# Stores of turned input-gradient leaf rows: from the SyncE queue to the GpSimd queue, with the order of all work planned anew

## The chip, the cores and the metric

The kernel runs on one core of a Trainium2 chip. The metric is the device time in microseconds (us) of one execution, the median of several runs. A core has five engines that work side by side, each through its own instructions in order: TensorE (PE: matmuls; its weight loads are listed as PEld), VectorE (DVE), ScalarE (ACT), GpSimd (POOL) and SyncE (SP). SP computes nothing: it issues transfers (DMAs) between the main memory and the on-chip memory. GpSimd can compute and can issue transfers as well. Whoever issues a transfer, 16 DMA engines of the core carry it out. Instructions of different engines wait for one another through semaphores; an instruction that waits holds up all that stand behind it on its engine.

## The reference

The reference is a strided 1-D convolution with group normalisation over time and GELU, and its gradients for all four inputs. With batch 2, time 16000, 256 channels in and out, K = 31 taps, stride 2 and L = 7985 output rows:

```python
h = sum(einsum('blc,cd->bld', x[:, i:i + 2 * L:2, :], w[i]) for i in range(31))
mu = h.sum(1) / L;  var = ((h - mu) ** 2).sum(1) / L
out = gelu(((h - mu) / sqrt(var + 1e-5)) * gn_gamma + gn_beta)      # tanh form
d_x, d_w, d_gamma, d_beta = vjp(out)(grad_out)
```

All arrays are bfloat16. The outputs are `out` and the four gradients.

## The kernel before

**Less multiplication, more addition.** The 31 taps, padded to 32, are split by nested sums and differences (three products where four would be needed, at several levels). A branch is called A, B or C at each level, and a pair of branch and leaf names one of nine leaf operands (`COMBOS`, L23). VectorE makes sums and differences of operand rows, TensorE multiplies leaf operands with leaf weights, ScalarE and VectorE spread and add partial results in PSUM.

**Stages.** F0 and F1 are the forward for batch 0 and batch 1 (`forward`, L908). GELU and its derivative for batch 0 (`gelu_batch`, L1063) run beside F1, those for batch 1 beside the first part of the input gradient. G0 and G1 are the input gradient for batch 0 up to its third chunk, and from its fourth chunk on (`input_grad`, L1453). W is the weight gradient (`weight_grad`, L1688). There are 4 chunks per batch, two halves (`pr`) per chunk in G, and three branches per half.

**The input gradient.** For each chunk `e_load` (L1205) loads the derivative rows (`dy_d`, in the trace `dyd`) and the forward's rows (`h_d`, `hd`); `e_comp` (L1213) turns them into the gradient before normalisation and spreads it into one of two buffers `ET`, with copies of a few halo columns on GpSimd (L1258) and memsets (L565). `g_sums` (L1284) makes the nine leaf operands of the chunk from it, matmuls (`g_mm`, L1335) use them, and `g_evac` (L1429) collects the result for a store to `out_1`.

**What the change touches.** The weight gradient needs the same nine leaf operands, but with time on the partitions. `dl_turn` (L1268) therefore turns each leaf by two transposing DMAs of 128 KB (`turn`, L558; in the trace L561, `arena<-arena`) into one of four row buffers `DNO` (L603), and stores the buffer's two halves with two DMAs of 128 KB in pieces of 512 bytes (`load`, L548; in the trace L556, `dld<-arena`) to the DRAM tensors `dl_d` (`dld`). Nine leaves in eight chunks make 72 leaves, 144 turns and 144 stores. `dl_turn` asks for GpSimd ("POOL"), but `load` overrides that: every transfer above 4096 bytes in a stage of `ONE`, which lists all stages, is issued by SP. The four buffers rotate, so the turns of a leaf wait until the stores of the leaf four earlier have landed. In W `d_tile` (L1561) loads those rows back.

**What else SP issues in these stages.** The loads of `e_load`; for GELU of batch 1, the loads of `hd`, the turns of `grad_out`, and the stores of `dyd` and `yd` (`gelu_unit`, L1100), where the buffer of `yd` is written again by ScalarE's L1110 in the next unit; the stores to `out_1`; and, towards the end, the first loads of `x` for W (L1541).

**What sets the order.** Nothing is emitted where it is written. `add` (L294) records every operation with its engine, an estimated duration, and the cells that it reads and writes. `order` (L323) gives each a due time: the place of the matmul that needs it, less durations, less a hand-kept lead for its kind (`lead`, and by chunk `fine`). `listing` (L341) then plays the engines through with the estimated costs, eight transfer slots for SP and eight for GpSimd among them, picks on each engine the ready operation that is due first, and `emit` (L465) issues all operations in the order of the starts that it found. A changed cost or lead can therefore move any instruction on any engine.

Of the kernel before, what the change touches and what calls it, by code (L numbers as in the profile page):

```python
# [12 lines left out]
ACT = mybir.ActivationFunctionType  # L13
# [25 lines left out]
class Plan:  # L39
# [3 lines left out]
    def __init__(self, tc):  # L43
# [10 lines left out]
            "F0 f_evac last": -14.5,  # L54
            "F0 f_mm f_leaf": -67.5,
            "F0 f_mm f_outer": 14.0,
            "F0 f_mm f_three_ac": -19.0,
            "F0 f_mm f_three_b": 56.0,
            "F0 f_mm pe_turn": -135.5,
            "F0 f_outer forward": -15.5,  # L60
            "F0 f_seed forward": -60.0,
            "F0 f_three_b f_first": -19.5,
            "F0 load f_evac": 62.5,
            "F0 load put": 10.5,
            "F0 tt f_sums": -97.0,
            "F0 tt second": 16.5,
            "F0 ve_neg f_seed": -25.0,
            "F0 w_sub f_first": 8.0,
            "F0 w_sum w2_part": 5.0,
            "F0 zero x_load": 16.5,  # L70
            "F1 f_evac last": -54.0,
            "F1 f_mm f_leaf": -235.5,
            "F1 f_mm f_three_ac": -3.5,
            "F1 f_mm f_three_b": -20.5,
            "F1 f_outer forward": 3.5,
            "F1 f_seed forward": 3.0,
            "F1 keep f_evac": 0.5,
            "F1 load f_evac": 60.5,
            "F1 load gelu_unit": 44.5,
            "F1 load out0_store": 57.0,  # L80
            "F1 tiny elem_finalize": 50.5,
            "F1 tiny fwd_stats": -72.0,
            "F1 tt f_sums": -41.0,
            "F1 tt gelu_unit": -21.0,
            "F1 tt second": -47.5,
            "F1 tt third": -63.5,
            "F1 turn gelu_batch": 21.5,
            "F1 turn gelu_unit": -5.0,
            "F1 turn x_load": 48.5,
            "F1 ve f_seed": -19.0,  # L90
            "G0 cp e_comp": 4.5,
            "G0 g_mm g_three_b": -9.0,
            "G0 g_three_b input_grad": 6.5,
            "G0 gelu_batch conv_stem_kernel": 3.5,
# [3 lines left out]
            "G0 load dgb_store": -3.5,  # L98
            "G0 load dl_turn": 8.0,
            "G0 load e_load": 22.5,  # L100
            "G0 load g_evac": 9.5,
            "G0 load load_w2": 29.5,
            "G0 plus g_seed": 5.0,
            "G0 tiny elem_finalize": -9.0,
            "G0 tt first": -48.0,
            "G0 tt gelu_unit": -0.5,
            "G0 tt second": 1.0,
            "G0 tt third": -113.0,
            "G0 turn dgb_store": 7.0,
            "G0 turn dl_turn": 1.0,  # L110
            "G0 turn gelu_batch": 5.5,
            "G0 w_sum load_w2": -47.0,
            "G0 zero e_comp": 7.0,
            "G0 zero gelu_batch": -54.0,
            "G1 cp e_comp": -94.5,
            "G1 e_comp e_load": 13.0,
            "G1 g_mm g_leaf": -2.0,
            "G1 g_mm g_outer": -7.5,
            "G1 g_mm g_three_ac": -8.0,
            "G1 g_mm g_three_b": -18.0,  # L120
            "G1 g_three_b input_grad": -201.5,
            "G1 keep g_evac": 3.5,
            "G1 keep g_seed": -2.0,
            "G1 load dl_turn": 11.0,
            "G1 load e_load": -6.0,
            "G1 load g_evac": -4.0,
            "G1 plus g_seed": 2.5,
            "G1 spread e_comp": -11.0,
            "G1 spread g_seed": -197.5,
            "G1 tt first": 3.5,  # L130
            "G1 tt second": -15.0,
            "G1 tt third": -13.0,
            "G1 turn dl_turn": 3.5,
            "G1 w_sum w2_outer": -21.5,
            "G1 zero e_comp": 1.0,
            "W keep w_keep": 4.5,
            "W keep weight_grad": 1.0,
            "W load d_tile": -32.5,
            "W load out0_late": 35.5,
            "W load w_emit": 13.5,  # L140
            "W load weight_grad": 39.0,
            "W load x_raw": 1.5,
            "W pair_d weight_grad": -3.5,
            "W pair_x weight_grad": 0.5,
            "W turn out0_late": -50.0,
            "W ve w_done": 8.5,
# [4 lines left out]
            "W w_emit w_done": 3.0,  # L151
            "W w_emit weight_grad": -196.0,
            "W w_mm w_leaf": 6.0,
            "W w_pairs weight_grad": -424.0,
# [5 lines left out]
            "F0 f_evac last": {0: 17.5, 3: -12.5},  # L160
            "F0 f_mm f_outer": {0: 37.5, 1: -12.5, 2: -135.0, 3: -49.5},
            "F0 f_mm f_three_ac": {0: -27.5, 1: -38.0, 2: -88.5},
            "F0 f_mm f_three_b": {0: 8.0, 1: -29.0, 2: -39.0, 3: -181.0},
            "F0 f_outer forward": {3: -15.0},
            "F0 f_seed forward": {3: 33.0},
            "F0 f_three_b forward": {0: -13.5},
            "F0 load f_evac": {2: 52.0, 3: -30.5},
            "F0 load put": {0: 22.0, 3: 20.5},
            "F0 tt f_sums": {0: -9.5, 1: 73.5, 2: 18.0},
            "F0 tt second": {1: -52.0, 2: -50.5},  # L170
            "F0 tt third": {1: 42.0, 2: -34.5, 3: 14.5},
            "F0 turn x_load": {0: 58.0, 2: 30.0},
            "F0 ve f_first": {0: -21.5},
            "F0 ve f_seed": {0: 24.0, 3: 1.0},
            "F0 ve_neg f_seed": {0: 88.5, 3: 58.5},
            "F0 w_sum w2_part": {1: 20.5, 2: 22.5},
            "F0 zero x_load": {3: 11.0},
            "F1 f_evac last": {3: -17.5},
            "F1 f_mm f_outer": {3: -41.0},
            "F1 f_mm f_three_ac": {1: -60.5, 3: -4.0},  # L180
            "F1 f_mm f_three_b": {2: 17.0},
            "F1 f_outer forward": {3: -9.5},
            "F1 f_seed forward": {3: 5.5},
            "F1 gelu_unit gelu_batch": {0: -26.0, 1: -15.0, 2: -22.0, 3: -74.0, 5: 11.5},
            "F1 keep f_evac": {3: 12.5},
            "F1 load f_evac": {3: -19.0},
            "F1 load gelu_unit": {2: 13.0, 3: -10.5, 5: -21.0, 6: -68.5},
            "F1 load out0_store": {0: 15.5, 1: 33.0, 2: 20.0, 3: 11.5, 4: -148.0, 5: -4.5, 6: 10.0, 7: 29.5},
            "F1 tiny elem_finalize": {0: -92.5},
            "F1 tiny fwd_stats": {0: 62.5},  # L190
            "F1 tt f_sums": {0: 3.0, 1: 46.0, 2: 30.0},
            "F1 tt gelu_unit": {2: 22.0, 4: 11.5},
            "F1 tt second": {0: -38.0, 2: 31.5},
            "F1 tt third": {3: 11.0},
            "F1 turn gelu_batch": {0: -185.0, 1: -49.0, 2: 30.5, 3: -58.0},
            "F1 turn gelu_unit": {0: -22.5, 1: -25.5, 2: -148.0, 3: -45.0, 5: 31.5, 6: -51.5, 7: -2.5},
            "F1 turn x_load": {1: 15.0, 2: 40.0, 3: -40.0},
            "F1 ve f_seed": {3: 29.0},
            "F1 w_sub f_again": {3: -37.5},
            "F1 zero f_evac": {3: -3.0},  # L200
            "G0 cp e_comp": {0: -151.0, 2: -2.5},
            "G0 e_comp e_load": {0: -17.5, 1: -8.0, 2: -8.5, 3: 7.0},
            "G0 g_mm g_leaf": {0: -2.0, 3: -173.5},
            "G0 g_mm g_three_ac": {1: -1.0, 3: 17.5},
            "G0 g_mm g_three_b": {0: -4.5, 1: 1.5, 2: -3.0},
            "G0 g_three_b input_grad": {0: 1.0, 1: 0.5, 3: 0.5},
            "G0 gelu_batch conv_stem_kernel": {6: 41.0},
            "G0 gelu_unit gelu_batch": {1: -8.0, 2: -3.0, 3: 2.5, 4: -7.0, 5: -4.5, 6: -3.0},
            "G0 keep g_evac": {0: -14.5, 2: -2.0},
            "G0 keep g_seed": {0: -4.0, 1: -1.5, 2: -1.0, 3: 2.5},  # L210
            "G0 load dgb_store": {0: -2.5},
            "G0 load dl_turn": {0: -28.0, 1: 1.5, 2: -8.5},
            "G0 load e_load": {0: -11.0, 1: -12.0, 2: 3.5},
            "G0 load g_evac": {0: -5.0},
            "G0 load gelu_unit": {0: 49.0, 1: 13.0, 2: 8.5, 3: -15.5, 5: -4.5, 6: -15.0},
            "G0 load load_w2": {3: -9.0},
            "G0 plus g_seed": {0: -2.5},
            "G0 spread e_comp": {0: 8.0, 1: -99.5, 2: 2.5, 3: -23.0},
            "G0 tiny elem_finalize": {0: 1.5},
            "G0 tt first": {2: 36.5},  # L220
            "G0 tt gelu_unit": {0: -36.5, 1: -1.5, 2: -40.0, 3: -10.0, 5: 2.5, 6: 2.0},
            "G0 tt second": {0: -72.0, 1: 7.0},
            "G0 tt third": {0: 99.5},
            "G0 turn dgb_store": {0: -5.5},
            "G0 turn dl_turn": {1: 1.0, 2: -2.0},
            "G0 turn gelu_batch": {0: 12.5, 2: 14.5, 3: 9.0, 4: -32.5, 5: 11.0, 6: -89.5, 7: -0.5},
            "G0 w_sum load_w2": {3: 24.5},
            "G0 zero e_comp": {2: 1.5, 3: 16.5},
            "G1 e_comp e_load": {1: 0.5},
            "G1 g_mm g_leaf": {0: -114.5, 3: -2.5},  # L230
            "G1 g_mm g_outer": {0: -8.5, 1: -9.0, 2: -2.5, 3: -1.5},
            "G1 g_mm g_three_ac": {0: -6.5, 1: -7.0, 2: -4.0, 3: -1.0},
            "G1 g_mm g_three_b": {0: 3.5, 1: 15.0, 2: 10.0, 3: 11.0},
            "G1 keep g_evac": {0: 1.5, 1: -1.0, 2: 4.5, 3: 1.0},
            "G1 load dl_turn": {0: -3.5, 1: -1.5},
            "G1 load e_load": {1: -2.0, 2: -0.5},
# [1644 lines left out]
```

## Time and profile before

| What | Value |
|---|---|
| Median of 3 runs | 1195.17 us (1194.51 to 1196.55) |
| Profiled execution, its own time | 1190.87 us |
| Its span, first to last instruction | 1189.1 us |
| Mean granted TensorE clock | 0.99 |
| DMA packets moved | 243.55 MB, 205 GB/s in the mean |
| SP's stores to `dld` | 144, of 128 KB |
| SP's turns of on-chip rows | 161 (144 of them leaf rows) |
| DMAs issued by GpSimd | 6, of 0.5 KB |

A profile row for a group reads: line, engine, operation, what is written and read, the count; then the busy time in us and the mean of one in ns; then the idle time of the engine before it and what ended that. Rows of SP are marked SPq: SP only issues, so a row's length is the time that the issue took, with what it waited for inside it. The chain of waits follows the work that ended last back in time, at each step to what released it; its rows have a start, a length and a name. In the view of windows a stretch is followed by its length and by the busy time and count of each engine, then by the granted TensorE clock (1.00 is full speed), the mean busy share of the 16 DMA engines and the rate in GB/s.

### The profile page before, as it was taken

What the parts mean: (1) busy time and instruction counts of PE and PEld (TensorE: products, weight loads), DVE (VectorE), ACT (ScalarE), POOL (GpSimd) and SP (SyncE); (2) the same over time, 40 slices, a digit from 0 to 9 for tenths busy, and PEclk for the clock granted to TensorE, in tenths of its full rate; (3) what the DMA queues carried; (4) which work ended last, traced back from release to release, by engine and by line L of the source; (5) the groups of instructions that cost most, each with busy time, mean ns of one, the idle gap of its engine ahead of it and who ended that gap; (6) DMA issues with size and microseconds to landing.
All of it is one profiled execution on the core that took longest, in us unless ns stands there. A gap on an engine that the chain in (4) does not pass through costs nothing.

```text
span 1189.1 us, 18747 instructions
## 1 busy us (share of the span) xinstructions
PE 1136.3 (96%) x7645; PEld 756.0 (64%) x7700; DVE 981.3 (83%) x861; ACT 568.9 (48%) x849; POOL 26.2 (2%) x77
## 2 busy tenths in 40 slices
PE   6999999999999999999898999999889999999998
PEld 3888899777777954444343444444368856666685
DVE  7998787799899988898584868868589999598995
ACT  1253454778876577987654657643322201211200
POOL 0000000000000010000000100000000000000000
PEclk8999999999999999999899999999999999999999
DMA  9476836979785789999769776676879735998755
GB/s 212 62 186 117 195 120 143 205 164 222 168 212 138 287 275 256 264 246 231 206 181 250 153 200 165 165 184 184 242 251 248 257 116 185 298 365 272 263 158 148
DMA packets 378061, 243.55 MB, mean 205 GB/s; under 512 B 233377, under 2 KB 353831, under 8 KB 373799
## 3 DMA queue, kind: packets, MB, share of 16 engines
q1 hardware_dynamic: 377783, 242.35, 76.4%
q8 instruction: 60, 0.98, 0.3%
q14 instruction: 26, 0.21, 0.1%
q0 software_dynamic: 192, 0.00, 0.0%
HBM read 106.24 MB, written 80.25 MB: 157 GB/s over the span
## 4 chain that ended last, share of the span: by engine, by line
PE 55%; DVE 14%; DMA 11%; SPq 9%; ACT 7%; issue 3%; DVEq 0%; ACTq 0%; another core or an unknown queue 0%
PE ps L750 21%; PE ps L1571 19%; PE ps L1338 16%; SPq L561 5%; SPq L556 4%; DMA arena<-in_x_dram 3%; DMA arena<-dld 2%; DVE arena L1125 2%; DVE arena L708 2%; DVE ps L1405 2%; DMA arena<-dyd 1%; DMA yd<-arena 1%; ACT arena L845 1%; DVE arena L1539 1%; ACT arena L1117 1%
## 5 line engine op out<-in xcount | busy, mean ns | idle before, releaser
L1338 PE MATMUL ps<-arena 128*128 128x512 bf16 (+1 forms) x1880 | 418.4, 380 | 26.7 <-ACT ps L1365 10.3
L750 PE MATMUL ps<-arena 128*128 128x256 bf16 (+4 forms) x3460 | 408.9, 282 | 12.2 <-DMA arena<-in_x_dram 5.5
L750 PEld LDWEIGHTS <-arena 128*128 128x128 bf16 x3460 | 339.2, 99 | 82.0 <-DMA arena<-in_x_dram 5.8
L1338 PEld LDWEIGHTS <-arena 128*128 128x128 bf16 x1920 | 189.2, 99 | 254.6 <-issue 39.9
L1571 PE MATMUL ps<-arena 128*128 128x256 bf16 (+1 forms) x2305 | 309.7, 296 | 9.9 <-DVE arena L1637 6.2
L1571 PEld LDWEIGHTS <-arena 128*128 128x128 bf16 x2320 | 227.6, 98 | 92.1 <-DVE arena L1637 7.0
L845 ACT ACTIVATE arena<-ps 128x1024 f32<-128x1024 f32 (+1 forms) x143 | 145.3, 1021 | 291.8 <-PE ps L1338 98.6
L708 DVE TENSOR_TENSOR arena<-arena 128x2064 bf16<-128x2064 bf16 (+7 forms) x126 | 156.3, 1266 | 32.7 <-PE ps L750 31.2
L1405 DVE TENSOR_TENSOR ps<-ps,arena 128x2048 f32<-128x2048 f32 x40 | 91.7, 2296 | 24.1 <-PE ps L1338 14.2
L1291 DVE TENSOR_TENSOR arena<-arena 128x1032 bf16<-128x1032 bf16 (+1 forms) x120 | 84.1, 727 | 30.5 <-PE ps L1338 24.7
L1125 DVE TENSOR_TENSOR arena<-arena 128x2048 bf16<-128x2048 bf16 (+1 forms) x80 | 95.7, 1196 | 13.4 <-ACT arena L1117 9.1
L1539 DVE TENSOR_TENSOR arena<-arena 128x4096 bf16<-128x4096 bf16 x38 | 86.1, 2286 | 21.0 <-DMA arena<-in_x_dram 20.1
L865 ACT ACTIVATE arena<-ps 128x512 bf16<-128x512 f32 (+1 forms) x64 | 37.1, 581 | 51.7 <-PE ps L750 46.6
L1666 ACT COPY ps<-ps 128x256 f32<-128x256 f32 x54 | 19.3, 357 | 71.4 <-PE ps L1571 69.6
L1405 DVE TENSOR_TENSOR arena<-ps,arena 128x2048 f32<-128x2048 f32 x16 | 36.6, 2288 | 16.2 <-ACT arena L845 12.8
L1724 DVE TENSOR_TENSOR arena<-arena 128x4608 bf16<-128x4608 bf16 x18 | 45.6, 2551 | 3.7 <-DMA arena<-dld 3.7
L1115 DVE SCALAR_TENSOR_TENSOR arena<-arena 128x2048 bf16<-128x2048 bf16 (+1 forms) x16 | 35.8, 2237 | 13.7 <-ACT arena L1112 13.7
L1650 DVE TENSOR_TENSOR arena<-arena 128x2048 bf16<-128x2048 bf16 x38 | 45.4, 1218 | 1.8 <-PE ps L1571 1.8
L820 ACT ACTIVATE arena<-ps 128x512 f32<-128x512 f32 x56 | 29.7, 599 | 33.5 <-PE ps L750 17.0
L786 ACT ACTIVATE ps<-ps 128x256 f32<-128x256 f32 x75 | 27.8, 371 | 33.9 <-PE ps L750 32.5
L1110 ACT ACTIVATE arena<-arena,stats 128x1024 bf16<-128x1024 bf16 (+1 forms) x32 | 37.7, 1210 | 11.5 <-DMA yd<-arena 8.6
L1240 ACT COPY arena<-arena 128x768 bf16<-128x768 bf16 (+1 forms) x64 | 36.5, 616 | 13.5 <-DVE arena L1231 12.8
(79 smaller groups left out, 644.1 us busy)
## 6 DMA issues: line engine op xcount, KB each, us to landing
arena<-in_x_dram SPq DMA_DIRECT2D x40, 1024.0 KB
dld<-arena SPq DMA_DIRECT2D x144, 128.0 KB
arena<-hd SPq DMA_DIRECT2D x32, 512.0 KB
out_dram<-arena SPq DMA_DIRECT2D x14, 1024.0 KB
arena<-dld SPq DMA_DIRECT2D x18, 640.0 KB
arena<-dld SPq DMA_DIRECT2D x18, 576.0 KB
vl<-arena SPq DMA_DIRECT2D x36, 256.0 KB
arena<-vl SPq DMA_DIRECT2D x9, 1024.0 KB
```

What stands on the lines that cost most here:

```text
L556: lambda: e.dma_start(out=out, in_=in_), dma=np_ * ns / 16e3 * 1.03, ns=ns, tp=SH[pk], slack=slack)
L561: lambda: nc.sync.dma_start_transpose(out=out, in_=in_), dma=np_ * PK[256] / 16e3 * 1.03, ns=PK[256], tp=SH[256], slack=slack)
L708: lambda: nc.vector.tensor_tensor(out=o, in0=a, in1=b, op=ALU.add))
L750: yield nc.tensor.matmul(ps[:, dh, cs], lhsT=wt, rhs=mv, start=s0, stop=False, skip_group_check=True)
L845: lambda: nc.scalar.activation(out=out, in_=ps, func=ACT.Copy, scale=scale))
L1125: add("DVE", dve(nf), [o], [a, b_], lambda: V.tensor_tensor(out=o, in0=a, in1=b_, op=op))
L1291: lambda: nc.vector.tensor_tensor(out=o, in0=a, in1=b, op=ALU.subtract))
L1338: yield nc.tensor.matmul(ps[:, e, 0:wide], lhsT=lt, rhs=mv, start=s0, stop=False, skip_group_check=True)
L1405: lambda: nc.vector.tensor_tensor(out=o, in0=a, in1=b, op=ALU.add))
L1539: add("DVE", dve(4096), [o], [a, b], lambda: nc.vector.tensor_tensor(out=o, in0=a, in1=b, op=ALU.add))
L1571: yield nc.tensor.matmul(ps[:, s, c0:c1], lhsT=lt, rhs=mv, start=s0, stop=False, skip_group_check=True)
L1724: add("DVE", dve(4608), [o], [u, v], lambda: nc.vector.tensor_tensor(out=o, in0=u, in1=v, op=ALU.subtract))
```

## The change

`load` gets a parameter `own`; with it the override by `ONE` does not apply. `dl_turn` passes it, so that GpSimd issues the 144 stores to `dld`. Three planner costs change with it: SP's time for one issue, SP's time for one turn, and the time from GpSimd's issue to the start of its transfer. All leads (`lead`, `fine`) are replaced by new ones, about 250 numbers of which the diff here shows two.

```diff
@@ Plan.__init__
         self.lead = {
-            "F0 f_evac last": -14.5,
-            "F0 f_mm f_leaf": -67.5,
+            "F0 f_evac last": -8.0,
+            "F0 f_mm f_leaf": -225.0,
...
@@ Plan.listing
-                air.append(dict(i=i, on=False, act=False, lane=turn[k], rem=o["dma"], tp=o["tp"], t0=end + 1.3))
+                air.append(dict(i=i, on=False, act=False, lane=turn[k], rem=o["dma"], tp=o["tp"], t0=end + (1.3 if e == "SP" else 2.8)))
@@ load, turn
-    def load(out, in_, nbytes, run, eng="SP", slack=None):
-        if plan.stage in ONE and nbytes > 4096:
+    def load(out, in_, nbytes, run, eng="SP", slack=None, own=False):
+        if plan.stage in ONE and nbytes > 4096 and not own:
             eng = "SP"
...
-        add(eng, {"POOL": 0.74, "SP": 0.42 + 0.00016 * np_, "ACT": 0.4}[eng], [out], [in_],
+        add(eng, {"POOL": 0.74, "SP": 0.46 + 0.00016 * np_, "ACT": 0.4}[eng], [out], [in_],
...
-        add("SP", max(1.3, 0.15 + 0.00125 * np_), [out], [in_],
+        add("SP", max(1.38, 0.15 + 0.0013 * np_), [out], [in_],
@@ dl_turn
                     load(dl_d[b][3 * MIR[br] + MIR[lf]][j, r0:r0 + 256, :].rearrange("(m p) d -> p m d", p=P), o[:, j], 131072, 512,
-                         "POOL")
+                         "POOL", own=True)
```

More of the change, by code (lines that the diff above doesn't have):

```diff
@@ L67, in __init__ @@
[L67 to L79, printed above, removed]
@@ new lines, in __init__ @@
+            "F0 f_mm f_three_ac": -9.5,
+            "F0 f_mm f_three_b": 47.5,
+            "F0 f_mm pe_turn": -242.5,
+            "F0 f_outer forward": -28.0,
+            "F0 f_seed forward": -34.0,
+            "F0 keep f_evac": -31.5,
+            "F0 load f_evac": 64.0,
+            "F0 load put": 57.5,
+            "F0 tt f_sums": -113.0,
+            "F0 tt second": 38.0,
+            "F0 tt third": 4.0,
+            "F0 turn w2_part": 28.0,
+            "F0 ve f_seed": -11.5,
+            "F0 ve_neg f_seed": -19.0,
@@ new lines, in __init__ @@
+            "F0 w_sub f_first": 53.5,
+            "F0 w_sum w2_part": -8.5,
+            "F1 f_evac last": -189.0,
+            "F1 f_mm f_leaf": -272.5,
+            "F1 f_mm f_outer": -4.5,
+            "F1 f_mm f_three_ac": -4.5,
+            "F1 f_mm f_three_b": -22.0,
+            "F1 f_outer forward": 35.0,
+            "F1 gelu_unit gelu_batch": 1.5,
+            "F1 load f_evac": 129.0,
+            "F1 load gelu_unit": 32.0,
+            "F1 load out0_store": 20.0,
+            "F1 tt f_sums": -103.0,
@@ L92, in __init__ @@
+            "F1 tt gelu_unit": -49.0,
+            "F1 tt second": -81.5,
+            "F1 tt third": -71.5,
+            "F1 turn gelu_batch": 18.5,
+            "F1 turn gelu_unit": 9.0,
+            "F1 turn x_load": 38.0,
+            "F1 ve f_seed": -48.0,
+            "F1 w_sub f_again": 20.0,
             "G0 g_mm g_three_b": -9.0,
             "G0 g_three_b input_grad": 6.5,
-            "G0 gelu_batch conv_stem_kernel": 3.5,
+            "G0 gelu_batch conv_stem_kernel": 27.0,
             "G0 gelu_unit gelu_batch": -0.5,
@@ L106, in __init__ @@
             "G0 tt gelu_unit": -0.5,
             "G0 tt second": 1.0,
[L108 to L110 removed]
+            "G0 tt third": -51.0,
+            "G0 turn dl_turn": 2.5,
             "G0 turn gelu_batch": 5.5,
[L112 to L115, printed above, removed]
+            "G0 w_sum load_w2": 2.0,
+            "G0 zero e_comp": 8.5,
@@ L169, in __init__ @@
[L169 to L179, printed above, removed]
@@ L189, in __init__ @@
[L189 to L197, printed above, removed]
@@ L208, in __init__ @@
[L208 to L215, printed above, removed]
+            "F0 f_evac last": {2: -27.5, 3: -25.0},
@@ new lines, in __init__ @@
+            "F0 f_mm f_outer": {0: 43.5, 2: -114.5, 3: -73.5},
+            "F0 f_mm f_three_ac": {0: -37.0, 1: -36.5, 2: -94.5, 3: 2.0},
+            "F0 f_mm f_three_b": {0: 23.5},
+            "F0 f_three_b f_first": {0: 34.5},
+            "F0 f_three_b forward": {0: 5.0},
+            "F0 keep f_first": {0: -104.0},
+            "F0 load load_w": {0: -14.0},
+            "F0 load put": {0: -8.5, 2: -20.0},
+            "F0 tt f_sums": {0: 10.5, 1: 85.0, 2: 78.5},
+            "F0 tt second": {0: -20.0, 1: -48.5, 2: -78.5},
@@ new lines, in __init__ @@
+            "F0 tt third": {2: -87.5, 3: 12.0},
+            "F0 turn x_load": {0: 69.0},
+            "F0 ve_neg f_seed": {0: 158.5, 2: 49.0, 3: 57.5},
+            "F0 w_sub f_first": {0: -61.5},
+            "F0 w_sum w2_part": {0: 15.0, 1: -17.5},
+            "F1 f_mm f_leaf": {1: 7.0, 2: -13.0},
+            "F1 f_mm f_outer": {3: -50.0},
+            "F1 f_mm f_three_ac": {3: -3.5},
+            "F1 f_mm f_three_b": {0: 26.5},
+            "F1 f_outer forward": {3: -38.5},
+            "F1 gelu_unit gelu_batch": {0: -49.5, 1: -117.0, 2: -117.0, 3: -5.0, 5: 1.0, 6: 25.0, 7: 11.5},
@@ new lines, in __init__ @@
+            "F1 load gelu_unit": {1: 12.0, 2: 30.5, 5: 64.0, 6: -78.0},
+            "F1 load out0_store": {0: -35.5, 4: -169.0},
+            "F1 tiny fwd_stats": {0: -3.5},
+            "F1 tt f_sums": {0: 64.0},
+            "F1 tt gelu_unit": {0: -89.0, 1: 52.5},
+            "F1 tt second": {1: 38.0},
+            "F1 turn gelu_batch": {0: -301.5, 1: 93.5},
+            "F1 turn gelu_unit": {0: 10.0, 1: -62.5, 2: -102.0, 5: 25.5, 6: 25.5},
+            "F1 turn x_load": {1: 36.5, 2: 20.5, 3: 23.5},
@@ L219, in __init__ @@
+            "G0 spread e_comp": {0: 8.0, 1: -114.0, 2: 3.0},
             "G0 tiny elem_finalize": {0: 1.5},
[L220 to L226, printed above, removed]
@@ new lines, in __init__ @@
+            "G0 tt gelu_unit": {0: -12.0, 1: -3.5, 2: -66.0, 3: -7.5, 5: 3.0, 6: 2.0, 7: 2.0},
+            "G0 tt second": {1: 7.0, 2: -24.5},
+            "G0 turn dgb_store": {0: 35.5},
+            "G0 turn dl_turn": {0: 0.5, 1: 1.0},
+            "G0 turn gelu_batch": {0: 12.5, 2: 15.5, 3: 13.0, 4: -39.0, 5: 10.5, 6: -44.0},
+            "G0 w_sum load_w2": {3: 0.5},
+            "G0 zero gelu_batch": {6: -85.0},
+            "G1 cp e_comp": {2: -14.0},
+            "G1 e_comp e_load": {1: 0.5},
@@ new lines, in __init__ @@
+            "G1 tt second": {1: -15.5, 2: -39.0},
+            "G1 tt third": {2: 33.0, 3: -137.5},
+            "G1 turn dl_turn": {0: 0.5, 2: 0.5},
+            "G1 w_sum w2_outer": {3: 46.0},
+            "G1 zero e_comp": {2: -8.0},
+            "W keep w_keep": {1: 7.0, 6: 7.0},
+            "W keep weight_grad": {0: -30.5},
+            "W leaf_d weight_grad": {1: -5.5, 2: -24.0, 6: -96.0, 8: -46.0},
+            "W load d_tile": {2: 16.5, 3: -12.5, 4: 44.0, 5: 13.5, 6: 24.5},
+            "W load out0_late": {0: -26.5, 8: -3.0},
@@ new lines, in __init__ @@
+            "W load w_emit": {6: 5.5, 7: -3.5, 8: 84.0},
+            "W load weight_grad": {7: 24.0},
+            "W load x_raw": {2: -2.0, 4: -0.5, 5: -54.5},
+            "W pair_d weight_grad": {0: 13.5, 2: 21.5, 3: 22.5, 4: 8.0, 5: 12.0, 6: 11.0, 8: 31.0},
+            "W pair_x weight_grad": {1: 2.0, 3: 3.0, 5: 1.5, 6: 7.0, 7: 2.5, 8: -79.5},
+            "W turn out0_late": {0: -29.5, 8: 6.5},
+            "W ve w_done": {2: 38.0},
+            "W ve weight_grad": {7: 12.5, 8: -86.0},
+            "W w_add weight_grad": {1: -3.5, 3: 9.5, 4: -34.0, 5: 1.5, 6: -6.5, 8: 36.5},
```

172 lines of the change are left out of this document (59 added, 113 removed).

## The prediction

> **What bounds the kernel now.** I read the page's shares first, then the stages, then the waits of TensorE, then the chain of waits around each long one. The page says that TensorE is nearly always busy and that the chain which ends last runs through SP's queue for 9%:
>
> ```profile
> span 1189.1 us, 18747 instructions
> PE 1136.3 (96%) x7645; PEld 756.0 (64%) x7700; DVE 981.3 (83%) x861; ACT 568.9 (48%) x849; POOL 26.2 (2%) x77
> PE 55%; DVE 14%; DMA 11%; SPq 9%; ACT 7%; issue 3%; DVEq 0%; ACTq 0%; another core or an unknown queue 0%
> ```
>
> The stages (the view of windows; after the stretch and its length come the busy times of PE, PEld, DVE, ACT and POOL, then the granted clock, the DMA share and GB/s) show where the missing 4% lie. The first stretch is the forward, the second the input gradient (G0 and G1), the third the weight gradient; below them are parts of the second.
>
> ```profile
> 22.55:423.00 400.45, 399.87 (x3394) 332.93 (x3397) 350.84 (x339) 234.53 (x435) 8.88 (x19) 0.99 0.73 172
> 423.00:871.00 448.00, 416.01 (x1877) 188.40 (x1912) 339.25 (x331) 276.42 (x322) 14.37 (x43) 0.98 0.82 215
> 871.00:1189.10 318.10, 309.67 (x2305) 227.60 (x2320) 275.16 (x174) 54.00 (x88) 0.53 (x1) 0.99 0.73 229
> ...
> 500.00:550.00 50.00, 47.49 (x218) 21.59 (x221) 44.38 (x49) 42.95 (x50) 2.63 (x11) 1.00 0.97 228
> 550.00:600.00 50.00, 43.28 (x186) 19.09 (x189) 35.30 (x31) 33.61 (x37) 1.53 (x7) 0.93 0.87 225
> 600.00:650.00 50.00, 45.19 (x202) 20.27 (x204) 30.00 (x47) 23.94 (x31) 1.24 (x4) 0.97 0.78 205
> ```
>
> The forward leaves TensorE 0.6 us idle in 400: nothing is to be won there. The input gradient leaves 32 us, and that is the stage in which all the stores of the change are issued. TensorE's waits in it, from its timeline (start, length, idle time before in brackets):
>
> ```profile
> 571.91 3.57 PE L1338 MATMUL ps<-arena 128*128 128x512 bf16 x8 [4.51 <-ACT ps L1365]
> 641.56 2.65 PE L1338 MATMUL ps<-arena 128*128 128x512 bf16 x7 [3.72 <-ACT arena L845]
> 665.04 1.25 PE L1338 MATMUL ps<-arena 128*128 128x512 bf16 x5 [1.30 <-DVE arena L1291]
> 715.61 0.59 PE L1338 MATMUL ps<-arena 128*128 128x512 bf16 x2 [0.62 <-ACT arena L845]
> 763.20 1.02 PE L1338 MATMUL ps<-arena 128*128 128x512 bf16 x4 [1.28 <-ACT arena L845]
> ```
>
> I call them A to E. They are 11.4 of the 32 us; the rest is shorter gaps behind ScalarE and VectorE and a wait for the next stage's first loads at its end, which the change does not touch directly. A and B cost more than their idle time, because the granted clock falls after them:
>
> ```profile
> 571.90:577.30 5.40, 5.39 (x13) 1.88 (x13) 1.71 (x2) 5.09 (x7) 0.00 (x0) 0.50 1.02 219
> 595.60:606.30 10.70, 10.70 (x49) 4.87 (x50) 9.69 (x10) 7.37 (x8) 0.00 (x0) 1.00 0.67 179
> 641.60:644.20 2.60, 2.60 (x7) 0.96 (x8) 1.07 (x2) 1.92 (x4) 0.38 (x2) 0.61 1.06 292
> ```
>
> At half clock for 5.4 us, 2.7 us of work is lost after A; at 0.61 for 2.6 us, 1.0 us after B. So A to E cost 4.51 + 2.7 + 3.72 + 1.0 + 1.30 + 0.62 + 1.28 = 15.1 us.
>
> Who is late in front of them? In the chain of waits before A, SP's queue is the only thing that moves for 18 us (the rows left out between 547.62 and 565.97 are all SP's or its gaps of 0.05 us):
>
> ```profile
> 547.62 4.58 SPq L561
> ...
> 565.97 3.12 DMA yd<-arena
> ...
> 571.38 0.49 ACT ps L1365
> ```
>
> A store of `yd` stood behind SP's other work; ScalarE's next step needed its buffer, and the copy L1365 that TensorE wanted stood behind that step. SP's own timeline shows what stood in those stretches, and the same before B, D and E, where the last entry is the `dyd` load that gradient rows are made of:
>
> ```profile
> 553.53 2.07 SPq L556 DMA_DIRECT2D dld<-arena  x2
> ...
> 627.18 2.17 SPq L556 DMA_DIRECT2D dld<-arena  x4
> 629.99 0.41 SPq L556 DMA_DIRECT2D dld<-arena  x1
> 631.81 0.53 SPq L556 DMA_DIRECT2D arena<-dyd  x1
> ...
> 690.86 0.58 SPq L556 DMA_DIRECT2D dld<-arena  x1
> 694.16 1.57 SPq L556 DMA_DIRECT2D dld<-arena  x3
> 696.35 0.91 SPq L556 DMA_DIRECT2D dld<-arena  x2
> ...
> 740.09 2.69 SPq L556 DMA_DIRECT2D dld<-arena  x5
> 749.41 0.54 SPq L556 DMA_DIRECT2D dld<-arena  x1
> 750.51 0.44 SPq L556 DMA_DIRECT2D dld<-arena  x1
> ```
>
> **The change, part by part.** *Removed from SP:* 144 stores of 128 KB.
>
> ```profile
> L556 SPq DMA_DIRECT2D dld<-arena x144: 359/493/2322, 456.9 to 851.5; - x144
> ...
> L561 SPq DMA_TRANSPOSE arena<-arena x161: 1188/1267/2579, 236.9 to 845.8; - x161
> ```
>
> 144 x 0.493 (median) = 71 us of SP's 395 us between the first and last of them. The 144 turns of leaf rows stay: 144 x 1.267 = 182 us. What the 71 us are worth is read only where SP is the chain. Before A: 2.07 us of stores go, and 4.51 shrinks to 2.4. Before B: 2.17 + 0.41 = 2.6, and 3.72 shrinks to 1.1. Before D: 0.58 + 1.57 + 0.91 = 3.1, more than the 0.62. Before E: 2.69 + 0.54 + 0.44 = 3.7, more than the 1.28. C I leave as it is. Idle time gone: 2.1 + 2.6 + 0.6 + 1.3 = 6.6 us. For the clock I take all of B's 1.0 (after the 1.28 us gap of E no fall is seen) and half of A's 2.7: 2.4. Together 9.0 us. Bounds: 6.6 if the clock still falls; 15.1 if all five go, since SP is late at these places also from stores issued earlier.
>
> *Added to GpSimd:* 144 issues, 24 small copies (L1258) and the memsets (L565) among them in its queue. The nearest rows are the few DMAs that it issues already (the second fence is the view of DMA issues; its last number is us from issue to landing):
>
> ```profile
> L1258 POOL COPY arena<-arena 128x12 bf16<-128x12 bf16 (+2 forms) x24 | 13.6, 590 | 104.4 <-DVE arena L1291 59.2 <-ACT arena L1240 43.6 <-DMA arena<-arena 1.6
> L1088 POOL DMA_DIRECT2D arena<-in_grad_out_dram x2 | 1.6, 812 | 0.6 <-POOL arena L565 0.6
> ```
>
> ```profile
> out_dram<-arena POOLq DMA_DIRECT2D x4, 0.5 KB, 4.0
> arena<-in_grad_out_dram POOLq DMA_DIRECT2D x2, 0.5 KB, 4.4
> ```
>
> L1088 moves 256 pieces as a leaf store does, so I take 0.81 us, between SP's own 0.49 and twice it, 1.6. 144 x 0.81 = 117 us of 395 on an engine that is 2% busy: nothing by itself. Queued behind a store that waits for its turn are the halo copies; at most 16 stores stand ahead of a group of them in the new order, 13 us of issue. No instruction waited for L1258 in the trace, and the copies stand over 100 matmuls (22 us at 219 ns, from the row of 49 in 10.70 us) ahead of the chunk that needs them. I take 0, and up to 3 us if stores wait long.
>
> *The wait that the change adds.* Four row buffers rotate: the turns of leaf n + 4 wait until both stores of leaf n have landed. The new order has runs of 14, 10, 12 and 11 turns on SP without anything between, where the old has at most 6. In such a run a buffer's round is two turns (2.53), a landing, two issues (1.62) and the store's landing X; SP issues four leaves in 10.14.
>
> ```profile
> 657.52 5.63 DMA arena<-arena
> ...
> 856.27 10.05 DMA arena<-in_x_dram
> ```
>
> ```profile
> SPq L561 <- DMA dld<-arena: 9.6, 6, 3.7
> ```
>
> For the turn's landing I take the 5.63 that the chain shows for such a transfer; SP already waited 9.6 us in 6 turns for stores. So SP waits 2.53 + 5.63 + 1.62 + X - 10.14 = X - 0.36 per run. X for 128 KB from GpSimd is not in the trace: at least the 4.4 of half a KB; above, the 10.05 us of the load at the stage's end. I take 4.4, the nearest row: 4.0 us, 16 in four runs. That gives back 16 of 71, 23% of the relief: 9.0 x 0.77 = 6.9 us.
>
> *Planned anew:* lead times and three costs (SP's issue 0.42 to 0.46, a turn 1.3 to 1.38, GpSimd's start of a transfer 1.3 to 2.8) change the order on all engines. In the weight gradient TensorE's order and the loads' places hardly move; in the forward by up to some eighty matmuls. Between a loss of 15 us (two gaps like A) and a gain of 2 I take 0, as nothing is idle in the forward.
>
> **Sum.** Profiled execution: 1190.87 us (span 1189.1 and 1.8 around it); 1190.9 - 6.9 = 1184.0. That execution lies 4.3 under the median of the runs, 1195.17; the same 6.9 off it is **1188.3**.
>
> A rule against it: the Trainium skill, "SBUF — State Buffer", section "Who interferes with whom", says that VectorE's two-port instructions lock GpSimd out, so that it cannot write its DMAs' descriptors. The candidates in this stage are like this row:
>
> ```profile
> L1220 DVE TENSOR_SCALAR arena<-arena,stats 128x2048 bf16<-128x2048 bf16 x10 | 8.0, 805 | 4.9 <-DMA arena<-hd 4.9
> ```
>
> By that page a store that meets one is late by at most one such 0.8 us, X is 5.2 and the gain 6.5 in place of 6.9; no row here shows such a meeting.
>
> **Rivals.** *Stores land late (slower).* The decision lies in X. Four leaves' stores cost SP 8 x 0.493 = 3.9 before, the run waits X - 0.36: above X = 4.3 a run is no faster than it was, and what stands behind it is later. At X = 8 each of four runs loses 7.6 - 3.9 = 3.7, 15 us, and the loads behind them hit TensorE fully; less 6.9 that the other places win, +8: 1203. For: DMA share 0.78 to 0.97 in these windows, and X taken sits on the threshold. Against: 97 of the 144 turns are not in such runs. Chance 0.25.
>
> *The new order opens gaps elsewhere (slower).* VectorE has 44 of 50 us in 500 to 550 and the forward has no slack: two gaps like A, 2 x 7.2 - 6.9 = +7.5: 1202.7. For: every lead changed. Against: the sequences are close. Chance 0.17.
>
> *The transfers bound A, not their issue.* At 0.97 and 0.87 the DMA engines are nearly full before A, and the bytes are the same: A stays, B, D and E give (2.6 + 1.0 + 0.6 + 1.3) x 0.77 = 4.2: 1190.9. The Trainium skill, "DMA: Bandwidth & Descriptors", section "Issuing engines are not separate DMA queues", says the same: issuing elsewhere saves issue time alone. Chance 0.12.
>
> That the change does nothing is excluded: all 144 stores are GpSimd's in the built program.
>
> **How the numbers follow.** Forecast 0.40, the transfers 0.12: faster 0.52. Slower 0.25 + 0.17 = 0.42. Between, where gain and waits cancel, 0.06; 0.2% (2.4 us) is about what the runs of this kernel can tell from no change. Range: 1180 (all five gaps gone, 15.1) to 1205 (both slower rivals and 2 us); outside I leave 0.2. Within the forecast alone: 1180 to 1189.
>
> **What would show it.** Right: no `dld` rows on SP, the stretches before 571, 641, 715 and 763 shorter, A and B under 2.5 us, the clock at 0.50 once less in the stage, SP's wait for `dld` stores under 30 us. Wrong: that wait above 40 us, landings of GpSimd's stores above 5 us, new TensorE waits above 2 us behind a `dyd` or `hd` load or in the forward.

## The result, and the profile after

| Runs (one chip each) | Before | Changed | Ratio, 95% interval |
|---|---|---|---|
| the change's own | 1195.84 us | 1176.70 us | 0.9838 [0.9816, 0.986] |
| second set of experiments | 1192.11 us | 1179.25 us | 0.9888 [0.9869, 0.9907] |
| third set of experiments | 1195.76 us | 1176.04 us | 0.985 [0.9819, 0.9882] |

The change makes the kernel 13 to 20 us faster. (The first set of experiments has the kernel before in it, at 1194.14 us, but not the changed one.) The prediction had the direction and the place, and a third to a half of the size: it forecast 6.9 us, to 1188.3, and 1176.7 lies below its range, 1180 to 1205. The intervals in the first two rows do not overlap; so kernels are compared below within one set only.

The page of the changed kernel, in the rows that answer to those of before (span; engines; the chain that ended last, by engine):

```profile
span 1174.9 us, 18909 instructions
PE 1133.9 (97%) x7700; PEld 755.0 (64%) x7700; DVE 980.1 (83%) x861; ACT 568.8 (48%) x849; POOL 128.3 (11%) x221
PE 84%; DVE 7%; ACT 4%; DMA 3%; issue 2%; SPq 0%; DVEq 0%; ACTq 0%
```

SP's queue has gone from the chain (9% before) and TensorE's own work has 84% of it (55%). The windows, forward, input gradient, then two parts of the latter:

```profile
22.55:423.00 400.45, 400.35 (x3406) 333.35 (x3404) 353.15 (x345) 236.30 (x439) 7.32 (x19) 1.00 0.72 175
423.00:871.00 448.00, 430.97 (x2068) 203.32 (x2067) 352.56 (x338) 278.77 (x325) 118.06 (x187) 0.99 0.85 220
...
550.00:600.00 50.00, 48.36 (x227) 22.18 (x227) 43.54 (x43) 36.74 (x40) 16.00 (x23) 1.00 0.90 211
600.00:650.00 50.00, 48.28 (x227) 22.05 (x226) 38.35 (x56) 22.86 (x33) 15.06 (x25) 1.00 0.82 217
```

In 423 to 871 TensorE is busy 431.0 us where it was 416.0; but after the change the last 20 us of this stretch belong to the weight gradient. Its first matmuls, before and after (idle time before in brackets):

```profile
871.02 1.25 PE L1571 MATMUL ps<-arena 128*128 128x256 bf16 x5 [5.46 <-DVE arena L1637]
```

```profile
851.27 23.89 PE L1559 MATMUL ps<-arena 128*128 128x256 bf16 x202 [4.87 <-DVE arena L1625]
```

So the input gradient's matmuls end at 865.56 before and at 846.40 after, 19.2 us earlier. The span shrank by 14.2 us only, because from its first matmul on the weight gradient took 318.1 us in the profiled execution of before and 323.6 in this one. In the profiles of all other runs it took 320.7 to 326.4, in either order; why it was short in that one execution is not known.

The idle time before the matmuls of the input gradient, from the pages, before and after:

```profile
L1338 PE MATMUL ps<-arena 128*128 128x512 bf16 (+1 forms) x1880 | 418.4, 380 | 26.7 <-ACT ps L1365 10.3
```

```profile
L1326 PE MATMUL ps<-arena 128*128 128x512 bf16 (+1 forms) x1920 | 415.6, 377 | 12.2 <-ACT ps L1353 5.0
```

In 550 to 600, where A was, it is busy 48.36 for 43.28, at a granted clock of 1.00 for 0.93. The DMA engines are as full as before there, 0.90 for 0.87. TensorE's own timeline has only four gaps left above 0.7 us between 540 and 640 (idle time before in brackets), and none of A's or B's kind:

```profile
550.65 1.89 PE L1326 MATMUL ps<-arena 128*128 128x512 bf16 x8 [0.74 <-ACT ps L1353]
...
581.79 26.50 PE L1326 MATMUL ps<-arena 128*128 128x256 bf16 x124 [0.73 <-DVE ps L1393]
609.00 18.73 PE L1326 MATMUL ps<-arena 128*128 128x512 bf16 x88 [0.71 <-ACT ps L1353]
...
638.39 54.83 PE L1326 MATMUL ps<-arena 128*128 128x512 bf16 x256 [0.71 <-ACT ps L1353]
```

The moved stores themselves (the tile's view: duration in ns, least/median/most; the time to landing), and what SP and GpSimd wait for (us, times, longest; the second fence is of the kernel before):

```profile
L544 POOL DMA_DIRECT2D dld<-arena x144: 723/723/1001, 440.0 to 835.5; - x144
...
DMA to landing us min/median/max: 2.2/3.9/8.9
```

```profile
SPq L561 <- DVE arena L1291: 20.1, 10, 5.8
```

```profile
SPq L549 <- DVE arena L1279: 34.8, 14, 8.7
...
SPq L549 <- DMA dld<-arena: 9.4, 9, 2.4
```

```profile
POOL dld L544 <- DMA arena<-arena: 248.6, 49, 21.7
```

GpSimd waits 249 us for turns, and the tile's view names nobody who waits for its issues. SP now waits longer for VectorE's leaf operands (L1279 is L1291 of before, `g_sums`): it has come up with its producers. Its wait for the stores' landing is 9.4 us, where it was 9.6.

### The profile page after: what moved, and what is told of

Its sections match the earlier page's. It is cut to its first block, busy times and chain, and to the rows that moved or that the text cites. A ratio compares the mean times of both kernels' runs of the same rounds, so it can differ in the third digit from the quotient of the medians.

```text
span 1174.9 us, 18909 instructions
## 1 busy us (share of the span) xinstructions
PE 1133.9 (97%) x7700; PEld 755.0 (64%) x7700; DVE 980.1 (83%) x861; ACT 568.8 (48%) x849; POOL 128.3 (11%) x221
## 4 chain that ended last, share of the span: by engine, by line
PE 84%; DVE 7%; ACT 4%; DMA 3%; issue 2%; SPq 0%; DVEq 0%; ACTq 0%
PE ps L738 32%; PE ps L1326 27%; PE ps L1559 25%; DMA arena<-in_x_dram 2%; DVE ps L1393 2%; ACT arena L833 1%; DVE arena L696 1%; DVE arena L1393 1%; DVE arena L680 1%; ACT ps L1353 0%; ACT arena L1098 0%; DVE arena L1625 0%; DVE arena L1103 0%; DMA out_dram<-arena 0%; ACT arena L1124 0%
## 5 line engine op out<-in xcount | busy, mean ns | idle before, releaser
L544 POOL DMA_DIRECT2D dld<-arena x144 | 104.7, 729 | 266.9 <-DMA arena<-arena 248.6
L1279 DVE TENSOR_TENSOR arena<-arena 128x1032 bf16<-128x1032 bf16 (+1 forms) x120 | 84.2, 725 | 21.9 <-PE ps L1326 16.1
L553 POOL MEMSET arena<- 128x128 bf16 (+11 forms) x40 | 8.4, 243 | 424.8 <-DVE arena L696 140.1
```

Source lines behind the costliest of these rows:

```text
L544: lambda: e.dma_start(out=out, in_=in_), dma=np_ * ns / 16e3 * 1.03, ns=ns, tp=SH[pk], slack=slack)
L1279: lambda: nc.vector.tensor_tensor(out=o, in0=a, in1=b, op=ALU.subtract))
```

## The experiments

Three theories. **T1:** SP's time to issue was the bound, and the gain is that time given back. **T2:** the newly planned order made the gain. **T3:** the stores fare better as transfers (a queue of their own, larger packets).

**First set: each half alone, time given back, one step further.** The move alone: the kernel before in its own order on every engine; only who issues differs.

```diff
-        e = {"SP": nc.sync, "POOL": nc.gpsimd, "ACT": nc.scalar}[eng]
+        e = {"SP": nc.sync, "POOL": nc.gpsimd, "ACT": nc.scalar}[issue or eng]
...
-                         "POOL")
+                         "POOL", issue="POOL")
```

> The kernel before with its own order on all other engines; only the 144 stores to dld are issued by GpSimd. T1 (SP's issue time, 71 to 86 us of it, made the late rows): the gaps A to E go without any new order, -10 to -17 us against the kernel before, and G's matmuls end 10 to 17 us earlier. T2 (the newly planned order made the gain): within 4 us of the kernel before, or slower, since the old order has its stores' places for SP. T3 (the stores fare better as transfers, in larger packets on a queue of their own): also -10 to -17; this run does not part T1 from T3.

Measured 1180.81 us against 1194.14, ratio 0.9885 [0.9859, 0.9912]. TensorE's idle time before L1338 falls from 26.7 us to 14.1, but SP waits 24.3 us for stores to land (9.6 before):

```profile
L1338 PE MATMUL ps<-arena 128*128 128x512 bf16 (+1 forms) x1920 | 417.3, 378 | 14.1 <-DVE ps L1405 5.7
```

```profile
SPq L561 <- DMA dld<-arena: 24.3, 8, 8.8
```

The order alone: the changed kernel without `own=True`.

```diff
-                         "POOL", own=True)
+                         "POOL")
```

> The changed kernel's leads and planner costs, but the 144 stores stay with SP. T1: SP is again 349 of 431 us busy in G, gaps of A's kind come back (elsewhere perhaps): within 4 us of the kernel before. T2: 12 to 19 us faster than it. T3: as T1.

Measured 1207.31 us, ratio 1.0109 [1.0089, 1.0129]: 13 us slower than before. All three theories missed this; T2 by most. The likely reason, not tried by itself, is that the new order has its places for a freer SP. With the stores back on it TensorE idles more than in the old order, 34.6 us for 26.7:

```profile
L1326 PE MATMUL ps<-arena 128*128 128x512 bf16 (+1 forms) x1920 | 420.7, 379 | 34.6 <-ACT arena L833 10.7
```

Time given back to SP, without the bytes: the changed kernel in its order, with a tiny DMA from SP beside each of GpSimd's stores.

```diff
+    def with_idle(out, in_):
+        yield nc.gpsimd.dma_start(out=out, in_=in_)
+        k = idle_n[0]
+        idle_n[0] += 1
+        yield nc.sync.dma_start(out=idle_d[k:k + 1, :], in_=zt2[0:1])
```

> The changed kernel in its own order; beside each of GpSimd's 144 stores SP issues one more DMA of 512 bytes, which nothing waits for. That gives SP back 144 x about 0.4 = 58 us of issue time and adds 74 KB, less than 0.1% of the bytes. T1: 8 to 17 us slower than the changed kernel, with gaps like A to E in G behind late yd stores and dyd loads. T2: within 2 us of it. T3: within 2 us of it.

Measured 1185.22 us, ratio 0.992 [0.9882, 0.9958]. Since it has to be set against the changed kernel, it ran again beside it in the third set:

> The changed kernel with one more DMA of 512 bytes from SP beside each store, which cost SP 57 us in its first run (144 of 0.40 us in the mean), beside the changed kernel on the same chip. T1: 4 to 10 us above the changed kernel. T3: within 2 us of it.

There it took 1186.54 us against 1176.04 of the changed kernel: 10.5 us more, for these issues (the tile's view of the first run; in the second the median is 310 ns) and for 74 KB:

```profile
L543 SPq DMA_DIRECT2D idle<-zt x144: 232/383/1436, 447.7 to 842.4; - x144
```

144 x 0.383 = 55 us of SP's time (45 in the second run), and hardly anything that waits for it: GpSimd did twice, 4.1 us in all. That is T1's price and speaks against T3, which expected nothing. TensorE's timeline in the second run has waits over 1.5 us at 622 and 647 again, behind ScalarE and VectorE:

```profile
622.20 10.52 PE L1335 MATMUL ps<-arena 128*128 128x512 bf16 x47 [1.62 <-ACT arena L842]
647.36 47.06 PE L1335 MATMUL ps<-arena 128*128 128x512 bf16 x215 [2.09 <-DVE ps L1402]
```

One step further: the 16 stores to `out_1` on GpSimd as well.

```diff
-                  ho[0:r].rearrange("p e k f -> p (e k f)"), r * 8192, 4096, "POOL", slack=60.0)
+                  ho[0:r].rearrange("p e k f -> p (e k f)"), r * 8192, 4096, "POOL", slack=60.0, issue="POOL")
```

> The changed kernel in its own order, with the 16 stores to out_1 in G issued by GpSimd as well (a possible better version). T1: SP is no longer the chain in G, so 16 x 0.5 = 8 us less of its time bring 0 to 2 us. T3: another 16 large stores on the second queue bring as much per byte as the 144 did, 2 us or more for each 18 MB, here some 2 to 3 us.

Measured 1182.24 us, ratio 0.99 [0.9881, 0.9919]: no better than the changed kernel in any set. As neither theory expected more than 3 us, this does not part them. There is one new gap of 5.49 us behind L1279 (TensorE's timeline). Ahead of it three turns took SP 12.45 us, where three medians are 3.8 (SP's timeline):

```profile
566.10 23.22 PE L1326 MATMUL ps<-arena 128*128 128x512 bf16 x100 [5.49 <-DVE arena L1279]
```

```profile
546.96 12.45 SPq L549 DMA_TRANSPOSE arena<-arena  x3
```

GpSimd had issued a 1 MB store to `out_1` at 542.12 (its timeline). That this store held the turns up is argued from the times alone. SP's wait for stores to `dld` is 24.5 us in this run, against 9.4 in the changed kernel.

**Second set: which stores, how many issues, and the row buffers.** The changed kernel ran again as a measure for the set:

> The changed kernel once more, beside the kernels of this set. Moving the stores alone, in the old order, gave 13.5 us (0.9885), the whole change 19 (0.9838), on different chips. T1: the ratio stays at 0.982 to 0.986, so that the new order is worth 3 to 7 us on top of the move, though it loses 13 us where SP keeps the stores. If the chips explain the difference, the ratio here is 0.987 to 0.990 and the new order is worth nothing.

0.9888 [0.9869, 0.9907]: the second expectation, by which the new order would be worth nothing. The third set takes that up. The stores of batch 0 alone, in the old order:

```diff
-                         "POOL", issue="POOL")
+                         "POOL", issue="POOL" if b == 0 else None)
```

> The kernel before in its old order, with GpSimd issuing only the 72 stores of batch 0, which fall before about 650 us; the 72 of batch 1 stay with SP. T1 (SP's backlog, largest around A and B, where SP is 22 to 25 of each 25 us busy): A, B and C go, D and E stay, -8 to -12 us. T3 (the stores as transfers): half the stores, half of the 13.5 us of the whole move, -6 to -7.

Measured 1182.74 us against 1192.11, ratio 0.9908 [0.9882, 0.9934]: half of the stores, 9.4 of the 12.9 us that the whole change brought in this set. A shrinks to 1.05 (now at 564.94) and B to 1.85 (at 630.07); a gap at E's place, where the stores stay on SP, remains:

```profile
564.94 17.46 PE L1338 MATMUL ps<-arena 128*128 128x512 bf16 x79 [1.05 <-ACT ps L1365]
630.07 1.02 PE L1338 MATMUL ps<-arena 128*128 128x512 bf16 x4 [1.85 <-ACT arena L845]
...
750.51 25.81 PE L1338 MATMUL ps<-arena 128*128 128x512 bf16 x110 [2.22 <-ACT arena L845]
```

Its counterpart, the stores of batch 1 alone (`b == 1`), ran in the third set:

> The kernel before in its old order, with GpSimd issuing only the 72 stores of batch 1, after about 640 us. Moving batch 0's gave 10.9 us on the earlier set. T1: D and E go, A and B stay, -1 to -5 us; the two halves sum to about the whole, 13 us. T3: -6 to -7, as much as the other half by the count.

Measured 1192.31 us against 1195.76, ratio 0.9988 [0.9966, 1.001]: between 4 us faster and 1 slower. A and B stand as they did:

```profile
571.21 20.08 PE L1338 MATMUL ps<-arena 128*128 128x512 bf16 x79 [4.34 <-ACT ps L1365]
641.59 3.15 PE L1338 MATMUL ps<-arena 128*128 128x512 bf16 x7 [4.46 <-ACT arena L845]
```

The same 72 x 0.49 us of SP are worth 9 us in one half and some 2 in the other. By T3, each half should have brought the same. The halves differ in one thing more: with batch 1's stores moved, SP waits 25.6 us for stores to land, with batch 0's 8.8 (9.6 before). So some 16 of the 35 us came back as waits:

```profile
SPq L561 <- DMA dld<-arena: 25.6, 11, 8.6
```

Fewer issues, same engine, bytes and piece size: one store per leaf in place of two, all on SP.

```diff
-                    load(dl_d[...][j, r0:r0 + 256, :].rearrange("(m p) d -> p m d", p=P), o[:, j], 131072, 512,
-                         "POOL")
+                    load(..., "POOL", fn=(lambda: iter(())) if j == 0 else (lambda d=dl_d[...].rearrange("j r d -> (j r) d")[34 + 512 * c:546 + 512 * c, :], o=o:
+                         nc.sync.dma_start(out=d.rearrange("(k p) d -> p k d", p=P), in_=o.rearrange("p j m d -> p (j m) d"))))
```

> The kernel before in its old order and with all stores on SP, but one DMA of 256 KB for a leaf in place of two of 128 KB: 72 issues, the same bytes in the same 512-byte pieces on the same queue. [...] T1: if such an issue takes 0.55 to 0.7 us, SP is 30 to 45 us freer in G and 4 to 9 us of the 13.5 come. T3: nothing, within 2 us of the kernel before.

(The merged rows land 512 in a row in `dld`, so the weight gradient reads other rows than it should and its values aren't the reference's. Of the 36 DMAs that clear rows of `dld`, 18 become longer, 34 rows each.) Measured 1183.53 us against 1192.11, ratio 0.9924 [0.9898, 0.995]. An issue of 256 KB costs SP hardly more than one of 128 KB (0.518 for 0.493 us, medians of the tile's view):

```profile
L1282 SPq DMA_DIRECT2D dld<-arena x72: 359/518/2050, 456.1 to 840.9; - x72
```

71 - 72 x 0.518 = 34 us of SP's time went, and 8.6 us of the total, without GpSimd, a second queue or larger packets. That speaks for T1, and T3 expected nothing. A and B do not go, though; they shrink to 2.79 and 2.03, and TensorE resumes 4.2 us earlier behind A (571.91 before) and 6.8 behind B (641.56):

```profile
567.74 19.15 PE L1338 MATMUL ps<-arena 128*128 128x512 bf16 x79 [2.79 <-ACT ps L1365]
634.72 1.02 PE L1338 MATMUL ps<-arena 128*128 128x512 bf16 x4 [2.03 <-ACT arena L845]
```

The row buffers: three in place of four, in the changed kernel's order.

```diff
-                o = ds[tbc[0] % len(ds)]
+                o, q = ds[tbc[0] % len(ds)], ds[tbc[0] % 3]
```

> The changed kernel in its own order, with three row buffers rotating in place of four: the turns of a leaf wait for the stores of the leaf three earlier. In a run of turns a buffer's round is 2.53 + 5.63 + 1.45 + 3.9 = 13.5 us against 7.6 of issue for three leaves. If a wait of SP for stores costs as the prediction priced it (SP's time is the gain, 9 us for 71 us of it), SP's wait grows from 9 to some 50 to 90 us and 5 to 12 us are lost. If SP has slack now, as T1 reads the trace after, the wait grows and the time moves by less than 4 us.

(The plan goes by `o`, the transfers use `q`. In an order made for four buffers some turns stand ahead of stores whose rows they then overwrite, so the weight gradient isn't the reference's, and such a store waits for the later turn.) Measured 1207.68 us, 28 us more than the changed kernel beside it:

```profile
SPq L549 <- DMA dld<-arena: 92.7, 25, 10.3
```

```profile
L1326 PE MATMUL ps<-arena 128*128 128x512 bf16 (+1 forms) x1880 | 419.2, 381 | 27.7 <-ACT ps L1353 15.4 <-DVE ps L1393 5.5 <-ACT arena L833 3.7
```

The wait grew as expected, but my reading of T1, that SP has slack for it now, is wrong: 79 us more of waiting than in the changed kernel beside it (92.7 for 14.0) cost 28. The wait that the prediction feared is a real price; with four buffers in this order little of it is incurred (9.4 to 14.0 us in three runs, 9.6 in the kernel before). As the overwritten rows add waits of their own, 28 us is no clean price of a buffer.

**Third set: what the new order adds to the move.** Both kernels side by side:

> The changed kernel beside the move alone on one chip: its first reading was 0.9838 of the kernel before, its second 0.9888, on two chips. If the new order is worth nothing on top of the move (as the prediction took it), it stands within 3 us of the move alone here; if it is worth 6 us, as the first readings of the two had it, 4 to 8 us below.

> The move alone in the old order, again. T1: 0.986 to 0.990 of the kernel before, whatever the changed kernel has on this chip; T2: more than 3 us above the changed kernel.

Measured 1176.04 us (1175.68 to 1178.7) for the changed kernel, 1179.54 (1177.17 to 1183.18) for the move alone, whose ratio to before is 0.9882 [0.9846, 0.9919]. The new order is worth some 3.5 us on top of the move; the two ranges overlap. TensorE's idle time in G says the same, 14.3 us against 17.5, here the changed kernel and then the move:

```profile
L1326 PE MATMUL ps<-arena 128*128 128x512 bf16 (+1 forms) x1880 | 413.5, 378 | 14.3 <-ACT ps L1353 5.0 <-DVE ps L1393 5.0 <-ACT arena L833 1.2
```

```profile
L1338 PE MATMUL ps<-arena 128*128 128x512 bf16 (+1 forms) x1880 | 413.8, 378 | 17.5 <-ACT ps L1365 6.1 <-DVE ps L1405 5.7 <-ACT arena L845 2.8
```

The move alone keeps three waits, at A's place, at B's and behind it, of 1.56, 1.26 and 1.31 us, which the new order does not have, and SP's wait for stores is 26.7 us in it, against 9.7:

```profile
SPq L561 <- DMA dld<-arena: 26.7, 10, 8.8
```

```profile
SPq L549 <- DMA dld<-arena: 9.7, 12, 2.3
```

That this wait is what makes those three gaps was not tried.

## Why the prediction was right in direction and short in size

**The bound and the place: right.** A to E were gaps of SP's making, the gain is in G, and A, B and the loss of clock behind them are gone.

**The step that failed: "Before A: 2.07 us of stores go, and 4.51 shrinks to 2.4", and the same for B.** It counts the stores that SP issues in the 18 us of the chain before the gap. But SP was late when that stretch began, from stores issued earlier. SP's timeline of the kernel before shows its last rest of over 1 us ahead of A, from 493.34 (492.94 + 0.40) to 496.76 (a wait for a store to land), and the tile's view, asked for two stretches, the stores that it issued from there to A, and from its rest up to 590.02 to B:

```profile
492.94 0.40 SPq L556 DMA_DIRECT2D yd<-arena  x1
496.76 2.85 SPq L561 DMA_TRANSPOSE arena<-arena  x2
```

```profile
L556 SPq DMA_DIRECT2D dld<-arena x20: 425/508/1226, 500.3 to 554.4; - x20
```

```profile
L556 SPq DMA_DIRECT2D dld<-arena x24: 404/495/607, 595.0 to 638.0; - x24
```

So 20 x 0.508 = 10 us of stores stand before A, not 2.07, and 24 x 0.495 = 12 us before B, not 2.6. This is the most that each stretch can give; what came lies between. The `yd` store ahead of A is issued at 565.97 in the kernel before. In the three runs of the old order with batch 0's stores on GpSimd (the move alone, twice, and batch 0 alone) it is issued at 559.84, 559.87 and 559.04, so 6.1 to 6.9 us earlier. Of these, 3.5 to 5.0 us are there already at the `yd` store before it (540.55, against 537.06, 535.93 and 535.59), ahead of the 18 us in which the prediction counted. The rest of the 10 us went into waits: from 496 to 572 SP waits 5.1 us for leaf operands in the first of these runs, 0.8 before. Nor does SP's queue alone carry the lateness. Further back the chain of the kernel before runs through landings of late `yd` stores, ScalarE and VectorE, and comes to SP at 547.62:

```profile
492.94 7.19 DMA yd<-arena
...
521.97 5.45 DMA yd<-arena
...
544.62 1.22 DVE arena L1138
547.62 4.58 SPq L561
```

In the three runs 0.24, 1.56 and 1.05 us are left of A's 4.51, and 2.10, 1.26 and 1.85 of B's 3.72. The prediction had a figure near the gain, 15.1 us "if all five go, since SP is late at these places also from stores issued earlier", and filed it as a bound. The move alone gave 13.3 and 16.2 us in the medians of its two sets (14.1 by the second ratio). That this is so close to 15.1 is in part luck, as these remains show. The experiments on the halves fit: where SP is without rest for 75 us (batch 0) its time is dear. In batch 1 it rests between (6.2 us up to 665.01, 4.6 up to 717.76) and waits more for landings, and moving as many stores brings about 2 us; how much each of the two does was not parted.

**The wait for four row buffers: 16 us predicted, hardly any in the changed kernel** (9.4 us in its first run, 14.0 and 9.7 in the others, 9.6 before). The store's landing was near, 3.9 us (median) for the 4.4 taken. The formula counts two issues twice: the turn's 5.63 us run from the start of its issue (in the chain and in SP's timeline it starts at 657.52), and a store's landing is counted from the start of its issue too. Without one turn's 1.27 and one store's 0.81 it gives 2.0 us for a run, 8 in all. Nor are the turns of a run issued back to back: in the four runs SP waits 10.0 us for VectorE (its waits, asked for by stretch), and the buffers come free meanwhile; for stores to land it waits 1.9 there. In the old order the wait did come, 24.3 and 26.7 us against 9.6 before, and the move still gave its 13 us and more. The factor 0.77 was wrong for the changed kernel.

**GpSimd: right.** 0.723 us an issue for the 0.81 taken, 104.7 us in all (117), and nobody waits for an issue.

**Planned anew, "I take 0": wrong in kind.** The order has no value of its own: it costs 13 us with the stores on SP, and with them on GpSimd it brings about 3.5, by ranges that overlap.

**The rivals.** *Stores land late:* the median landing, 3.9, stayed under the 4.3 us from which it was to decide, though single stores took up to 8.9. *The transfers bound A:* refuted; A went with the DMA engines at 0.90, and the merged stores brought 8.6 us with the same bytes in the same pieces on the same queue. *New gaps elsewhere:* none above 2 us in the forward; TensorE's idle time there is 0.1 us in 400. The Trainium skill's "DMA: Bandwidth & Descriptors", section "Issuing engines are not separate DMA queues", says that issuing elsewhere saves issue time alone. The runs agree; as far as they part the causes, that time was the gain of the move. The Trainium skill's "SBUF — State Buffer", section "Who interferes with whom", says that VectorE's two-port instructions can hold up GpSimd's descriptors. The issues show no sign of it: the longest of the 144 took 1.001 us against a median of 0.723. Why some stores took 8.9 us to land was not looked into.

**Left open:** the 0.5% between the first two readings of the change, how much of the new order's 3.5 us is the shorter wait for buffers, and why the weight gradient was short in the profile of before.

## What to carry to other kernels

When a queue that only issues is late, count all that could leave it since it last stood idle, not what stands in the last stretch before the gap. That is the most that it can give: here 6 to 7 of 10 us came, and the rest went into waits for producers. The gap itself shrinks by less than the queue gains, as TensorE also comes to it earlier. Look at the count of issues before their bytes: merging two stores into one cost SP 0.518 us for twice 0.493 and brought 8.6 us on the same queue. An order planned for one placement of the issues is to be judged with that placement only.

## What the runs showed of the hardware

The same stores left SP in pieces of 512 bytes and GpSimd in larger ones. The pages, before and after:

```profile
DMA packets 378061, 243.55 MB, mean 205 GB/s; under 512 B 233377, under 2 KB 353831, under 8 KB 373799
```

```profile
DMA packets 345806, 243.56 MB, mean 207 GB/s; under 512 B 233377, under 2 KB 316967, under 8 KB 341543
```

Between 512 bytes and 2 KB 36864 packets are gone, 256 for each of the 144 stores; between 2 and 8 KB there are 4608 more, 32 for each. The engines' time did not fall with the count. The queues' rows (packets, MB, share of 16 engines' span), before and then after:

```profile
q1 hardware_dynamic: 377783, 242.35, 76.4%
```

```profile
q1 hardware_dynamic: 338615, 223.47, 71.5%
q0 software_dynamic: 7104, 18.89, 5.7%
```

0.764 x 1189.1 - 0.715 x 1174.9 = 68 us left the one queue and 0.057 x 1174.9 = 67 us came to the other, for 18.9 MB either way: an eighth of the data packets, about the same time. In the profiles of the changed kernel's two other runs 65 and 68 us left and 73 and 70 came, so the figures are good to some 5 us.
